# The second product of the last three token tiles by Strassen's scheme, with the order of work behind it placed anew

## The chip, the cores and the metric

The kernel runs on one core of a Trainium2 chip. The metric is device time in microseconds (us) of one launch. A core has engines that work side by side, each with a queue of its own in program order: PE (TensorE, matrix products; its weight loads are listed as PEld), DVE (VectorE), ACT (ScalarE), POOL (GpSimd) and SP (SyncE, here only an issuer of DMAs). They share SBUF, from which they work; PE writes its results to the banks of PSUM.

## The reference

Local attention with a few global positions, and on its result a block of two dense layers. There are 8 batches, 8 heads, 576 positions, 64 columns a head:

```python
mask = (abs(pos[:, None] - pos[None, :]) <= 32) | is_global[:, None] | is_global[None, :]
scores = where(mask, scale * q @ k.T, -1e9)
attn = softmax(scores) @ v                    # [8, 8, 576, 64]
x = attn.transpose(0, 2, 1, 3).reshape(4608, 512)
h = x @ w_in                                  # 512 x 2048
g = softplus(h)
out = g @ w_out                               # 2048 x 512, float32
```

The second product, g @ w_out, is what the change is about.

## The kernel before

The 4608 tokens are worked in nine tiles m = 0 to 8 of TT = 512 tokens (`add_moe`). Attention runs ahead of them in 36 units n, four to a tile. One unit goes through all engines: scores on PE (tile s, L1128), mask added on DVE (st, L1132), row maximum on DVE (m, L1145), its subtraction on POOL (L1151), exponential on ACT (L1168), sum and reciprocal on DVE (sm L1175, rs L1177), the product with the reciprocal on POOL (pn<-st,rs, L1183), a transpose on DVE (pt, L1192). When the four transposes of a tile are there, PE makes the attention's result (xo, L1294, about 150 small matmuls), which ACT and DVE copy into xT (L777). Rows of global positions have a small product of their own (ov, L1052; odd).

Then comes the dense block of the tile. `first` (L1331) makes h in 16 groups of 4 matmuls of 512 columns, and `soft` on ACT (L1337) turns each group into a tile g of bf16, 128 of the 2048 inner values by 512 tokens. `second` (L1342) takes four blocks of 128 tokens; each block sums 16 matmuls of 512 columns in one PSUM bank, with a weight load of g ahead of each. `oev` (L777) copies the sums to SBUF (osb) on ACT or DVE, and `store` (L1354) writes 256 KB to DRAM: POOL's queue for tiles 0 to 5 (m < OWN), ACT's for tiles 6 to 8. The last block of tile 8 is done in two halves of 256 columns. Exponential and softplus each need ACT to load a table when it goes from one to the other.

The order of all this on each engine is no result of queues meeting at run time. The class `_Order` collects jobs with their dependencies, and `o.follow(ORDER)` gives each its place from a long tuple of numbers: a number divided by 5 is the job, its remainder the engine (PE, ACT, DVE, POOL, DMA). Each engine then runs its jobs strictly as they were placed, waiting on semaphores where a job's inputs come from another engine. So PE places matmuls of tile m's second product among those of tile m + 1's first one, and around xo. `run` also knows a flag `port=True`: a DVE job with it that is placed later than a POOL job is put behind it where their estimated times overlap; a POOL job is only looked at where it starts inside a DVE job that was placed already.

Of the kernel before, what the change touches and what calls it, by code (L numbers as in the profile page):

```python
# [334 lines left out]
def kernel(  # L335
# [984 lines left out]
    def add_moe(m, exps):  # L1320
        nt = TT

        def lo_of(c, n):
# [14 lines left out]

        def second(e, ns, kf, a, z):
            if kf == 0:  # L1340
                PS["o", m, ns, a] = psum(("o", m, ns, a), [P, z - a], FP32)
            nc.tensor.matmul(out=PS["o", m, ns, a][:, :], lhsT=PS["g", m, kf][:, ns * P:(ns + 1) * P],  # L1342
                             rhs=w_out_t[kf // 4][:, kf % 4, a:z], start=(kf == 0), stop=(kf == KF - 1))
# [178 lines left out]
```

## Time and profile before

| | |
|---|---|
| median of 3 runs | 327.88 us (326.84 to 328.69) |
| span of the profiled execution | 325.7 us |
| between that span and the median | 2.2 us |
| TensorE busy, granted clock | 97% of the span, 1.000 |
| VectorE, ScalarE, GpSimd busy | 69%, 71%, 62% |
| matmuls in all, of them of the second product | 5099, 592 |

The profile is of one execution; it has no time of its own besides its span, which counts from the first instruction to the last, so what a launch has around that is in the 2.2 us. Matmuls are pipelined, and a PE that is shown as busy is not therefore at its peak. The releaser of a wait is the engine whose signal came last. A slice of the page is a fortieth of the span, 8.1 us; tile 6 begins with its xo at 228.9 us, tile 7 at 261.6, tile 8 at 289.4, and the last matmul ends at 322.6.

### The profile page before, as it was taken

The page shows a single profiled execution, that of the slowest core. Times are in us where ns is not written, and L with a number is a line of the kernel's source. Part 1 is how long each engine was busy: PE and PEld are TensorE (multiplying, and loading weights), DVE is VectorE, ACT ScalarE, POOL GpSimd, SP SyncE. Part 2 cuts the span into 40 slices and gives each one's busy share as a digit, 9 for nine tenths or more (in the row PEclk, how much of TensorE's full clock was granted, in tenths as well). Part 3 has the DMA queues.
Part 4 walks back from the last instruction along what each step waited for, and adds up shares of the span by engine and source line. Part 5 has one row for each costly group of instructions (what it writes and reads, how often), then busy time and mean ns, then how long its engine had stood idle before and what let it go on. Part 6 is the DMA issues. An engine that isn't in the chain of part 4 may idle for free.

```text
span 325.7 us, 11720 instructions
## 1 busy us (share of the span) xinstructions
PE 315.4 (97%) x5099; PEld 174.8 (54%) x5099; DVE 225.9 (69%) x399; ACT 231.1 (71%) x471; POOL 200.6 (62%) x182
## 2 busy tenths in 40 slices
PE   8887999989999999999999999999999999999996
PEld 7556974565565655544455445445544454454453
DVE  6898479994899799988687978678755792530000
ACT  7897784768599787789558964695789468824621
POOL 8980759974678498596759962988556428420000
PEclk9999999999999999999999999999999999999999
DMA  8999799999887999999960899440202101000112
GB/s 211 160 176 223 171 192 162 173 214 201 137 138 125 173 189 169 221 176 175 194 132 36 158 156 192 107 137 10 94 0 99 47 24 64 0 34 34 64 38 92
DMA packets 168652, 41.52 MB, mean 127 GB/s; under 512 B 153114, under 2 KB 165658, under 8 KB 168602
## 3 DMA queue, kind: packets, MB, share of 16 engines
q1 hardware_dynamic: 151048, 25.96, 45.4%
q0 software_dynamic: 15680, 11.67, 19.7%
q10 hardware_dynamic: 1874, 3.15, 2.5%
q8 instruction: 40, 0.66, 0.9%
q14 instruction: 10, 0.08, 0.1%
HBM read 36.70 MB, written 9.44 MB: 142 GB/s over the span
## 4 chain that ended last, share of the span: by engine, by line
PE 72%; DMA 9%; DVE 9%; SPq 6%; POOL 2%; issue 1%; ACT 0%; POOLq 0%
PE o L1342 31%; PE h L1331 31%; SPq L494 5%; DMA wout<-in_moe_w_out_dram 4%; PE xo L1294 3%; DMA stage<-in_q_dram 3%; PE s L1128 3%; DMA stage<-in_k_dram 2%; PE ov L1052 2%; DVE m L1143 1%; DVE pt L1192 1%; PE pick L942 1%; DVE sm L1175 1%; DVE pn L1183 1%; POOL wout L1398 1%
## 5 line engine op out<-in xcount | busy, mean ns | idle before, releaser
L1342 PE MATMUL o<-wout,g 128*128 128x512 bf16 (+1 forms) x592 | 139.0, 374 | 0.0
L1331 PE MATMUL h<-xT,win 128*128 128x512 bf16 (+3 forms) x832 | 138.0, 314 | 0.7 <-DVE xT L777 0.4
L1337 ACT ACTIVATE g<-h 128x512 bf16<-128x512 f32 (+3 forms) x208 | 84.7, 481 | 32.1 <-PE h L1331 29.5
L1331 PEld LDWEIGHTS <-win 128*128 128x128 bf16 x832 | 70.3, 98 | 56.9 <-issue 1.6
L1342 PEld LDWEIGHTS <-g 128*128 128x128 bf16 x592 | 55.9, 98 | 61.0 <-issue 1.7
L1151 POOL TENSOR_TENSOR st<-st,m 128x1024 f32<-128x1024 f32 x32 | 60.4, 1898 | 34.1 <-DVE m L1145 34.0
L1183 POOL TENSOR_TENSOR pn<-st,rs 128x1024 bf16<-128x1024 f32 (+1 forms) x33 | 60.5, 1841 | 27.9 <-DVE rs L1177 20.2
L1132 DVE TENSOR_TENSOR st<-s,mask 128x512 f32<-128x512 f32 x64 | 41.0, 679 | 13.5 <-PE s L1128 13.4
L1175 DVE TENSOR_REDUCE sm<-st 128x8 f32<-128x1024 f32 x32 | 38.3, 1197 | 14.1 <-ACT st L1168 14.1
L1145 DVE TENSOR_REDUCE m<-st 128x8 f32<-128x1024 f32 x32 | 38.2, 1206 | 0.2
L1168 ACT ACTIVATE st<-st 128x1024 f32<-128x1024 f32 x32 | 33.1, 1054 | 6.2 <-POOL st L1151 6.0
L777 ACT COPY osb<-o 128x512 f32<-128x512 f32 (+1 forms) x28 | 16.1, 580 | 22.3 <-PE o L1342 20.1
L1192 DVE STREAM_TRANSPOSE pt<-pn 128x512 int32<-128x512 int32 x36 | 24.5, 688 | 9.0 <-POOL pn L1183 9.0
L777 ACT CAST xT<-xo 128x512 bf16<-128x512 f32 (+3 forms) x33 | 12.8, 458 | 20.1 <-PE xo L1294 20.1
L777 POOL CAST qk<-stage 128x1152 bf16<-128x1152 f32 (+2 forms) x14 | 17.2, 1248 | 8.6 <-PE xo L1294 7.9
L1337 ACT ACT_TABLE_LOAD x15 | 19.2, 1283 | 0.3
L1168 ACT ACT_TABLE_LOAD x14 | 18.0, 1283 | 0.2
L777 POOL CAST vb<-stage 128x1152 bf16<-128x1152 f32 x11 | 12.6, 1147 | 5.8 <-DMA stage<-in_v_dram 3.5
L774 POOL TENSOR_SCALAR qk<-stage 128x1152 bf16<-128x1152 f32 (+1 forms) x9 | 12.0, 1330 | 6.1 <-PE s L1128 3.7
L1354 POOL DMA_DIRECT2D out_dram<-osb x24 | 13.8, 574 | 3.0 <-DVE osb L777 1.6
L1294 PE MATMUL xo<-pt,vb 32*64 32x96 bf16 (+2 forms) x1328 | 14.1, 210 | 1.3 <-issue 1.3
L777 DVE CAST xT<-xo 128x512 bf16<-128x512 f32 (+3 forms) x19 | 9.9, 549 | 7.7 <-PE xo L1294 7.6
(128 smaller groups left out, 298.0 us busy)
## 6 DMA issues: line engine op xcount, KB each, us to landing
stage<-in_k_dram SPq DMA_DIRECT2D x48, 144.0 KB, 4.0
stage<-in_q_dram SPq DMA_DIRECT2D x48, 144.0 KB, 4.0
stage<-in_v_dram SPq DMA_DIRECT2D x48, 144.0 KB, 3.4
out_dram<-osb POOLq DMA_DIRECT2D x24, 256.0 KB, 3.4
out_dram<-osb ACTq DMA_DIRECT2D x11, 256.0 KB, 2.0
stage<-in_q_dram SPq DMA_DIRECT2D x4, 512.0 KB, 5.6
stage<-in_k_dram SPq DMA_DIRECT2D x4, 512.0 KB, 7.4
win<-in_moe_w_in_dram POOLq DMA_DIRECT2D x8, 256.0 KB, 6.4
```

The lines of the kernel that those rows point to most:

```text
L777: {"ACT": nc.scalar.copy, "DVE": V.tensor_copy, "POOL": nc.gpsimd.tensor_copy}[e](out, in_)
L1132: V.tensor_tensor(out=PS["st", n][:, h, :, :], in0=PS["s", n, h][:, :, :], in1=mask[:, h, j0:j0 + PB, :, :].rearrange("p j s i -> p j (s i ...
L1145: V.reduce_max(out=m[:], in_=flat(PS["st", n], h0, h1), axis=AX)
L1151: on(e).tensor_tensor(out=t, in0=t, in1=over(PS["m", n, y][:], SL * BL), op=OP.subtract)
L1168: nc.scalar.activation(out=t, in_=t, func=AF.Exp)
L1175: V.reduce_sum(out=sm[:], in_=flat(PS["st", n], h0, h1), axis=AX)
L1183: on(e).tensor_tensor(out=PS["pn", n][:, :, :, h0:h1].rearrange("p x s h -> p h x s"), in0=PS["st", n][:, h0:h1], in1=PS["rs", n, y][:].re ...
L1192: V.transpose(out=bass.AP(base.tensor, base.offset, ap=[list(base.ap[0]), [2 * STEP, PB // 2], [STEP + BL // 2, 2], [1, SL * BL]]), in_=PS ...
L1294: nc.tensor.matmul(out=PS["xo", v_, c][h * D:(h + 1) * D, (x - X0) * BL:(z - X0) * BL], lhsT=lhs, rhs=rhs, start=start, stop=stop)
L1331: nc.tensor.matmul(out=h[:, :], lhsT=w_in_t[c // 4][:, kd, c % 4 * P:(c % 4 + 1) * P], rhs=PS["xT", m][:, kd, lo:hi], start=(kd == 0), sto ...
L1337: nc.scalar.activation(out=PS["g", m, c][:, lo:hi], in_=PS[key][:, lo_of(c, hi - lo)], func=AF.Softplus)
L1342: nc.tensor.matmul(out=PS["o", m, ns, a][:, :], lhsT=PS["g", m, kf][:, ns * P:(ns + 1) * P], rhs=w_out_t[kf // 4][:, kf % 4, a:z], start=( ...
```

## The change

For tiles 6, 7 and 8 (m >= FAST = 6) the second product is cut into quarters: the 512 tokens in two halves, the 2048 inner values in two halves y of 1024, the 512 output columns in two halves. Instead of the eight products of quarters, seven are made, of sums and differences of quarters, by Winograd's form of Strassen's scheme:

- Of w_out: T0 to T3 in bf16, each in two halves p of 128x1024, once for all three tiles. They lie in the staging buffers of q and k, which are free when the last batch is cast. Four of these eight operations are on DVE, four on POOL.
- Of g: S1 to S4, each in two halves p, for every tile. S1 goes to the staging buffer of v, S3, S2 and S4 overwrite quarters of g. S3 overwrites a quarter that S1 reads, S2 overwrites one that S3 reads and needs S1, S4 reads S2: a chain S1, S3, S2, S4. S2 waits besides for product 1, which reads the quarter that S2 overwrites, and S4 for product 2. Of the 24, 16 are on DVE, 8 on POOL.
- Each of the seven products (L1444 in the new file) is 16 matmuls of 256 columns, 8 inner steps by 2 blocks of tokens. Products 1, 6, 7, 4 add up in one PSUM bank, which is copied out after each of them (four evictions on ACT or DVE); product 2 has a bank, 5 and then 3 a third one, and three operations on DVE (`total`, L1469) add them from PSUM onto the copied sums. Product 1 needs no S; 5 needs S1, 6 S2, 7 S3, 3 S4; 5, 6, 7, 4 need T0 to T3.
- Stores of these tiles go through SP's queue as 256 tokens by 256 columns (256 KB, pieces of 1 KB).
- g is one tile of 16 parts instead of 16 tiles, with the same waits part by part.
- The order is kept for the first 3438 matmuls on PE; from about 189.8 us of the profile before on, every job is placed anew.

```diff
@@ ORDER
-        6527, 5817, 5185, 5470, 4588, 7249, 5475, 5480, 5190, 5762, 5768, 5195, 5200, 5681, 5485, 5726, 6437, 5732, 5205, 5738, 5375, 5821, 5140, 5210,
+        6527, 5817, 5185, 5470, 4588, 7304, 5475, 5480, 5190, 5762, 5768, 5195, 5200, 5681, 5485, 5726, 6437, 5732, 5205, 5738, 5375, 5821, 5140, 5210,
...
-    gp = ctx.enter_context(tc.tile_pool(name="moe_g", bufs=1))
+    gs_ = const([P, KF, TT], BF16, "g")
...
-        for ns in range(nt // P):
+        if m >= FAST:
+            add_fast(m, own[0])
+        for ns in range(nt // P if m < FAST else 0):
...
+    FAST = 6
+    KH, NH, DH = KF // 2, TT // 2, d_model // 2
+    fast = [flat(stage[w]).bitcast(BF16)[:, y * KH * DH:(y + 1) * KH * DH].rearrange("p (k n) -> p k n", k=KH) for w in range(2) for y in range(2)]
+    s1 = flat(stage[2]).bitcast(BF16)[:, 0:KH * NH].rearrange("p (k n) -> p k n", k=KH)
...
+    def combine(e, out, a, b, op):
+        on(e).tensor_tensor(out=out, in0=a, in1=b, op=op)
...
+        cost = {"DVE": (620, 700), "POOL": (1905, 1905)}
...
+        bank_of = {1: "a", 6: "a", 7: "a", 4: "a", 2: "b", 5: "c", 3: "c"}
...
+            for n in range(2):
+                nc.tensor.matmul(out=PS[key][:, n, :], lhsT=A[i](k, slice(n * P, (n + 1) * P)), rhs=Bs[i](k), start=i in new and k == n == 0, stop=k == KH - 1 and n == 1, skip_group_check=i not in new)
...
+        def total(e, i, x):
+            V.tensor_tensor(out=PS["osb", m, i][:], in0=PS["o", m, x][:], in1=PS["osb", m, i][:], op=OP.add)
+            send(i)
...
+            nc.sync.dma_start(out=out[n0:n0 + NH, c * DH:(c + 1) * DH].rearrange("(n p) d -> p n d", p=P), in_=PS["osb", m, i][:])
...
+            add_s(1, p, lambda e, p=p: combine(e, sp(p), gq(p, 0, 1), gq(p, 1, 1), SUB), lo + hi, g(0, p) + g(1, p) + ([("s1", m)] if p else []),
+                  [] if p else [("s1", ("s1", m))])
+            add_s(3, p, lambda e, p=p: combine(e, gq(p, 0, 1), gq(p, 0, 1), gq(p, 0, 0), SUB), [S_[1, p]], g(0, p))
+        u1 = add_evict(0, add_product(1, []))
+        add_total(0, "b", [add_product(2, []), u1])
+        for p in range(2):
+            add_s(2, p, lambda e, p=p: combine(e, gq(p, 0, 0), gq(p, 0, 0), sp(p), SUB), [S_[3, p], P_[1, 4 * p + 3]], g(0, p) + [("s1", m)])
+            add_s(4, p, lambda e, p=p: combine(e, gq(p, 1, 0), gq(p, 1, 0), gq(p, 0, 0), SUB), [S_[2, p], P_[2, 4 * p + 3]], g(0, p) + g(1, p))
```

In PE's own order the seven products of tiles 6 and 7 are still spread: products 1, 2 and part of 5 among the tile's own h groups or behind them, 6 and 7 between the last h and the next tile's xo, 4 and 3 behind that. Tile 8 has all seven behind its last h group: product 1, then pieces of 5 and 2, 6, the rest of 2, 7, 5, most of 4, 3, the end of 4.

Three places of the new order matter. The first is DVE after tile 6's h, up to the attention that tile 7 waits for. A row is the line, the operation and its tiles (lines are lower by one or shifted in the new file: L1176 is L1175 of before). It was, before:

```order
L1175 TENSOR_REDUCE sm<-st 128x8
L1177 RECIPROCAL rs<-sm 128x8
L1070 TENSOR_TENSOR odd<-ov,odd 128x129
L1072 RECIPROCAL grs<-odd 128x1
L1192 STREAM_TRANSPOSE pt<-pn 128x2x2x128
L1175 TENSOR_REDUCE sm<-st 128x8
L1177 RECIPROCAL rs<-sm 128x8
L1192 STREAM_TRANSPOSE pt<-pn 128x2x2x128
L1132 TENSOR_TENSOR st<-s,mask 128x512 x4
L1145 TENSOR_REDUCE m<-st 128x8
L1192 STREAM_TRANSPOSE pt<-pn 128x2x2x128
```

There every row belongs to the attention. It is now, with stage_62 as the place of S1 and L1402 as the line of the new sums:

```order
L1176 TENSOR_REDUCE sm<-st 128x8
L1178 RECIPROCAL rs<-sm 128x8
L1402 TENSOR_TENSOR stage_62<-g 128x1024
L1402 TENSOR_TENSOR g<-g 128x4x256
L1402 TENSOR_TENSOR stage_62<-g 128x1024
L1402 TENSOR_TENSOR g<-g 128x4x256
L1402 TENSOR_TENSOR g<-g,stage_62 128x4x256
L1193 STREAM_TRANSPOSE pt<-pn 128x2x2x128
L1176 TENSOR_REDUCE sm<-st 128x8
L1178 RECIPROCAL rs<-sm 128x8
L778 COPY odd<-ov 64x129 x2
L1193 STREAM_TRANSPOSE pt<-pn 128x2x2x128
```

Five S of tile 6 (two S1, two S3, one S2) stand in one row ahead of a transpose and of the sum and reciprocal from which POOL's last pn of the tile is made. On POOL stood, at the same place before:

```order
L1151 TENSOR_TENSOR st<-st,m 128x1024
L1354 DMA out_dram<-osb 128x512 x2
L1183 TENSOR_TENSOR pn<-st,rs 128x2x512
L1354 DMA out_dram<-osb 128x512
L1183 TENSOR_TENSOR pn<-st,rs 128x2x512 x2
L1151 TENSOR_TENSOR st<-st,m 128x1024 x4
```

and now:

```order
L1152 TENSOR_TENSOR st<-st,m 128x1024
L1353 DMA out_dram<-osb 128x512
L1184 TENSOR_TENSOR pn<-st,rs 128x2x512
L1402 TENSOR_TENSOR g<-g,stage_62 128x4x256
L1184 TENSOR_TENSOR pn<-st,rs 128x2x512 x2
L1402 TENSOR_TENSOR g<-g 128x4x256
L1152 TENSOR_TENSOR st<-st,m 128x1024
L1353 DMA out_dram<-osb 128x512
L1402 TENSOR_TENSOR g<-g 128x4x256
```

An S2 (g<-g,stage_62) now stands between two pn, and two S4 behind them. The third place is DVE from tile 7's S to the end of the next attention:

```order
L1402 TENSOR_TENSOR stage_62<-g 128x1024
L1402 TENSOR_TENSOR g<-g 128x4x256
L1193 STREAM_TRANSPOSE pt<-pn 128x2x2x128
L778 COPY osb<-o 128x512
L1402 TENSOR_TENSOR stage_62<-g 128x1024
L1402 TENSOR_TENSOR g<-g 128x4x256
L1402 TENSOR_TENSOR g<-g,stage_62 128x4x256
L1176 TENSOR_REDUCE sm<-st 128x8
L1178 RECIPROCAL rs<-sm 128x8
L1193 STREAM_TRANSPOSE pt<-pn 128x2x2x128
L1469 TENSOR_TENSOR osb<-o,osb 128x512
L1193 STREAM_TRANSPOSE pt<-pn 128x2x2x128
```

Here too the sum and reciprocal for the last pn of tile 8's attention stand behind S, and two transposes behind those.

More of the change, by code (lines that the diff above doesn't have):

```diff
@@ L740 @@
         SLOTS[f"g{c}"] = 1
+    SLOTS["s1"] = 1
     KINDS = dict(h=(4, 0), o=(3, 0), o0=(4, 0), s=(4, 0), tr=(4, 0), pick=(2, 0), sg=(2, 0), ov=(2, 0), xo=(4, 0), gi=(1, 0))
@@ L1334, in soft @@
         def soft(e, c, key, lo, hi):
-            if lo == 0:
-                PS["g", m, c] = gp.tile([P, nt], BF16, tag=f"g{c}", name=f"g{c}")
-            nc.scalar.activation(out=PS["g", m, c][:, lo:hi], in_=PS[key][:, lo_of(c, hi - lo)], func=AF.Softplus)
+            nc.scalar.activation(out=gs_[:, c, lo:hi], in_=PS[key][:, lo_of(c, hi - lo)], func=AF.Softplus)
         def second(e, ns, kf, a, z):
@@ L1341, in second @@
                 PS["o", m, ns, a] = psum(("o", m, ns, a), [P, z - a], FP32)
-            nc.tensor.matmul(out=PS["o", m, ns, a][:, :], lhsT=PS["g", m, kf][:, ns * P:(ns + 1) * P],
+            nc.tensor.matmul(out=PS["o", m, ns, a][:, :], lhsT=gs_[:, kf, ns * P:(ns + 1) * P],
                              rhs=w_out_t[kf // 4][:, kf % 4, a:z], start=(kf == 0), stop=(kf == KF - 1))
@@ new lines, in add_sums @@
+    def add_sums():
+        cost = {"DVE": (620, 700), "POOL": (1905, 1905)}
+        SUB, ADD = OP.subtract, OP.add
+        t = lambda y, p: fast[y][:, 4 * p:4 * p + 4, :]
+        for p in range(2):
+            deps = had(("w_out", p), ("w_out", 2 + p))
+            for y, (a, b, op) in enumerate(((lambda p: wq(p, 0, 1), lambda p: wq(p, 0, 0), SUB), (lambda p: wq(p, 1, 1), lambda p: t(0, p), ADD),
+                                            (lambda p: wq(p, 1, 1), lambda p: wq(p, 0, 1), ADD), (lambda p: wq(p, 1, 0), lambda p: t(1, p), SUB))):
+                T["T", y, p] = o.add(cost, lambda e, y=y, p=p, a=a, b=b, op=op: combine(e, t(y, p), a(p), b(p), op),
+                                     deps + ([T["T", 0, p]] if y == 1 else [T["T", 1, p]] if y == 3 else []), rank=60, port=True)
@@ new lines, in add_fast, with gq, sp, product @@
+    def add_fast(m, mine):
+        if ("T", 0, 0) not in T:
+            add_sums()
+        SUB = OP.subtract
+        cost = {"DVE": (620, 700), "POOL": (1905, 1905)}
+        N = slice(0, NH), slice(NH, 2 * NH)
+        def gq(p, y, x):
+            return gs_[:, y * KH + 4 * p:y * KH + 4 * p + 4, N[x]]
+        def sp(p):
+            return s1[:, 4 * p:4 * p + 4, :]
+        g = lambda y, p: [("g", m, y * KH + 4 * p + k) for k in range(4)]
+        A = {1: lambda k, n: gs_[:, k, n], 2: lambda k, n: gs_[:, KH + k, n], 3: lambda k, n: gs_[:, KH + k, n],
+             4: lambda k, n: gs_[:, KH + k, slice(NH + n.start, NH + n.stop)], 5: lambda k, n: s1[:, k, n],
+             6: lambda k, n: gs_[:, k, n], 7: lambda k, n: gs_[:, k, slice(NH + n.start, NH + n.stop)]}
+        Bs = {1: lambda k: wq(k // 4, 0, 0)[:, k % 4], 2: lambda k: wq(k // 4, 1, 0)[:, k % 4], 3: lambda k: wq(k // 4, 1, 1)[:, k % 4],
+              4: lambda k: fast[3][:, k], 5: lambda k: fast[0][:, k], 6: lambda k: fast[1][:, k], 7: lambda k: fast[2][:, k]}
+        bank_of = {1: "a", 6: "a", 7: "a", 4: "a", 2: "b", 5: "c", 3: "c"}
+        new = (1, 2, 5)
+        used = {1: 0, 2: 1, 3: 1, 4: 1, 5: None, 6: 0, 7: 0}
+        P_ = {}
+        S_ = {}
+        def product(i, k):
+            key = ("o", m, bank_of[i])
+            if i in new and k == 0:
+                PS[key] = psum(key, [P, 2, DH], FP32)
+            for n in range(2):
+                nc.tensor.matmul(out=PS[key][:, n, :], lhsT=A[i](k, slice(n * P, (n + 1) * P)), rhs=Bs[i](k), start=i in new and k == n == 0, stop=k == KH - 1 and n == 1, skip_group_check=i not in new)
+        def add_product(i, after):
+            key = ("o", m, bank_of[i])
+            last = None
+            for k in range(KH):
+                deps = list(after) if last is None else [last]
+                deps += {1: lambda: [mine["soft", k], T["w_out", k // 4]], 2: lambda: [mine["soft", KH + k], T["w_out", 2 + k // 4]],
+                         3: lambda: [S_[4, k // 4]], 4: lambda: [mine["soft", KH + k], T["T", 3, k // 4]], 5: lambda: [S_[1, k // 4], T["T", 0, k // 4]],
+                         6: lambda: [S_[2, k // 4], T["T", 1, k // 4]], 7: lambda: [S_[3, k // 4], T["T", 2, k // 4]]}[i]()
+                last = o.add(mm(2, DH), lambda e, i=i, k=k: product(i, k), deps, rank=6, ins=4, opens=[("o", key)] if i in new and k == 0 else [],
+                             uses=([] if i in new and k == 0 else [key]) + ([("s1", m)] if used[i] is None else [("g", m, used[i] * KH + k)]))
+                P_[i, k] = last
+            return last
+        def add_s(i, p, fn, deps, uses, opens=()):
+            T["S", m, i, p] = S_[i, p] = o.add(cost, fn, deps, rank=10 * m + 2, port=True, uses=uses, opens=opens)
+        def evict(e, i):
+            PS["osb", m, i] = op.tile([P, 2, DH], FP32, tag="osb", name="osb")
+            copy(e, PS["osb", m, i][:], PS["o", m, "a"][:])
+            if i == 3:
+                send(i)
+        def total(e, i, x):
+            V.tensor_tensor(out=PS["osb", m, i][:], in0=PS["o", m, x][:], in1=PS["osb", m, i][:], op=OP.add)
+            send(i)
+        def send(i):
+            r, c = ((0, 0), (0, 1), (1, 1), (1, 0))[i]
+            n0 = m * TT + r * NH
+            nc.sync.dma_start(out=out[n0:n0 + NH, c * DH:(c + 1) * DH].rearrange("(n p) d -> p n d", p=P), in_=PS["osb", m, i][:])
+        def add_evict(i, dep):
+            return o.add(either(512), lambda e: evict(e, i), [dep], rank=3, opens=[("osb", ("osb", m, i))], uses=[("o", m, "a")])
+        def add_total(i, x, deps):
+            return o.add({"DVE": dve(512)}, lambda e: total(e, i, x), deps, rank=3, uses=[("osb", m, i), ("o", m, x)])
+        for p in range(2):
+            lo, hi = ([mine["soft", y * KH + 4 * p + k] for k in range(4)] for y in range(2))
+            add_s(1, p, lambda e, p=p: combine(e, sp(p), gq(p, 0, 1), gq(p, 1, 1), SUB), lo + hi, g(0, p) + g(1, p) + ([("s1", m)] if p else []),
[3 more added lines that the diff above has]
+        add_total(0, "b", [add_product(2, []), u1])
+        for p in range(2):
+            add_s(2, p, lambda e, p=p: combine(e, gq(p, 0, 0), gq(p, 0, 0), sp(p), SUB), [S_[3, p], P_[1, 4 * p + 3]], g(0, p) + [("s1", m)])
+            add_s(4, p, lambda e, p=p: combine(e, gq(p, 1, 0), gq(p, 1, 0), gq(p, 0, 0), SUB), [S_[2, p], P_[2, 4 * p + 3]], g(0, p) + g(1, p))
+        u2 = add_evict(1, add_product(6, [u1]))
+        u3 = add_evict(2, add_product(7, [u2]))
+        T["second", m] = add_evict(3, add_product(4, [u3]))
+        c22 = add_total(2, "c", [add_product(5, []), u3])
+        add_total(1, "c", [add_product(3, [c22]), u2])
@@ L1489 @@
         make_batch(batches(us)[-1] + 1)
-    o.follow(ORDER)
+    for key in list(T):
+        if key[0] == "T":
+            T[key]["deps"] += T["cast", B - 1, 0] + T["cast", B - 1, 1]
+        elif key[0] == "S" and key[2] == 1:
+            T[key]["deps"] += T["cast", B - 1, 2]
+    if ORDER:
+        o.follow(ORDER)
     for job in o.run(dict(PE=1200 if WARM else 3000, ACT=2600, DVE=2100, POOL=3400, DMA=2000)):
```

2 lines of the change are left out of this document (added), and 54 rows, old and new, of the table ORDER.

## The prediction

> **What bounds the kernel now.** I read the page's busy shares and its 40 slices first, then the chain of waits in order of time, then busy time by stage.
>
> ```profile
> span 325.7 us, 11720 instructions
> PE 315.4 (97%) x5099; PEld 174.8 (54%) x5099; DVE 225.9 (69%) x399; ACT 231.1 (71%) x471; POOL 200.6 (62%) x182
> PE   8887999989999999999999999999999999999996
> DVE  6898479994899799988687978678755792530000
> POOL 8980759974678498596759962988556428420000
> PE 72%; DMA 9%; DVE 9%; SPq 6%; POOL 2%; issue 1%; ACT 0%; POOLq 0%
> ```
>
> TensorE is busy 97% of the span and carries 72% of the chain; the change works from slice 23 on, where PE stands at 9 throughout while VectorE and GpSimd stand at 5 to 9 until tile 8 begins. Other engines' work is free there as long as PE never waits for it.
>
> ```profile
> 189.78 5.50 PE o L1342 x25
> 300.98 6.04 PE h L1331 x28
> 309.62 13.00 PE o L1342 x74
> 322.62 0.02 issue
> 322.64 0.37 ACT osb L777
> ```
>
> ```profile
> L1342 PE MATMUL o<-wout,g 128*128 128x512 bf16 x46 | 10.4, 379 | 0.0
> L1342 PE MATMUL o<-wout,g 128*128 128x256 bf16 x28 | 3.5, 273 | 0.0
> ```
>
> The first fence is the chain: a matmul of 512 columns every 6.04/28 = 0.2157 us. The second groups the matmuls after 309.6 by shape: the 74 of the chain's 13.00 us are 46 of 512 columns and 28 of 256. 46 x 0.2157 = 9.92, so the 28 took 3.08, 0.110 each. If half the columns were exactly half the time, it would be 0.108.
>
> ```profile
> 190.00:230.00 40.00, 40.00 (x669) 19.80 (x669) 30.60 (x50) 26.17 (x42) 27.09 (x20) 1.00 0.58 122
> 230.00:262.00 32.00, 32.00 (x433) 15.09 (x419) 21.63 (x36) 22.55 (x33) 18.85 (x14) 1.00 0.14 51
> 262.00:290.00 28.00, 28.00 (x361) 13.54 (x334) 14.87 (x21) 20.23 (x29) 13.76 (x8) 1.00 0.08 29
> ```
>
> These are stages of the end (stretch, length, then busy time of PE, PEld, DVE, ACT, POOL, granted clock, DMA share, GB/s). From 190 to 290 DVE has 33 us free and POOL 40 of 100, so the 40 new operations fit by their sum. The question is whether the last one before a product, or before the next tile's attention, ends in time.
>
> **What the matmuls save.** A tile's second product was 64 x 0.2157 = 13.80 us; it becomes 112 matmuls of 256 columns, 12.32 at 0.110 or 12.10 at 0.108. That is 1.5 to 1.7 a tile, 4.4 to 5.2 for three (tile 8 had 32 of its matmuls halved already, which changes nothing at this pitch). I take -4.9. The number of weight loads rises by 128 with the matmuls; at 98 ns each
>
> ```profile
> L1342 PEld LDWEIGHTS <-g 128*128 128x128 bf16 x592 | 55.9, 98 | 61.0 <-issue 1.7
> ```
>
> they stay under 0.108, and PEld is under half busy: 0, covered by the matmuls themselves.
>
> **Waits that go.** The small pieces of PE's work in that stretch:
>
> ```profile
> 195.28 1.56 PE xo L1294 x146
> 261.68 1.59 PE xo L1294 x153
> 222.08 0.80 PE L1052 MATMUL ov<-vb,pgt 32*32 32x129 bf16 x72
> 222.81 3.63 PE L1342 MATMUL o<-wout,g 128*128 128x512 bf16 x16
> 254.86 0.75 PE L1128 MATMUL s<-kx,qx 64*32 64x128 bf16 x64
> ```
>
> From 189.78 to the end at 322.64 the order has 279 matmuls of 512 columns at L1342 (60.2), 32 of 256 (3.5), 256 of L1331 (55.2), four xo groups (6.4), 288 scores s (3.0 at the last row's pace, less its drain), two ov (0.73 each, 222.08 to 222.81) and small picks (about 1.4): 131.2 of 132.9. So 1.3 to 1.7 us are waits spread over that stretch; they lie at the places where I now count whole new waits, and I take -1.3.
>
> **The combinations.** 8 T once, 24 S (8 a tile), each 128x1024 bf16 out of two bf16 tiles in SBUF; 20 on DVE, 12 on POOL. No such instruction is in the trace. Nearest rows:
>
> ```profile
> L1183 DVE TENSOR_TENSOR pn<-st,rs 128x512 bf16<-128x512 f32 x5 | 3.4, 718 | 0.0
> L1151 POOL TENSOR_TENSOR st<-st,m 128x1024 f32<-128x1024 f32 x32 | 60.4, 1898 | 34.1 <-DVE m L1145 34.0
> L777 DVE COPY kx<-qkg 128x320 bf16<-128x320 bf16 x2 | 0.5, 243 | 0.1
> L1183 DVE TENSOR_TENSOR pn<-st,rs x2: 1274/1898/2522, 65.8 to 67.0; 128x1024 bf16<-128x1024 f32 x2
> L777 POOL CAST qk<-stage x14: 403/1469/2477, 7.9 to 207.5; 128x1152 bf16<-128x1152 f32 x9, 128x512 bf16<-128x512 f32 x4, 128x256 bf16<-128x256 f32 x1
> ```
>
> On POOL: 1.90. On DVE: at most 1.27, the fp32 operation of the same 1024 columns at its fastest; the bf16 copy of 320 columns at 0.24 says that narrow types can go at more than double pace, about 0.5 for 1024. I take 0.70, nearest to the fp32 row with half the columns, which moves as many bytes. The Trainium skill gives the same for two-input bf16 operations ("VectorE: DVE Perf Modes", The perf-mode tier table): twice the pace of fp32, 1224 ns for 2048 columns; by it an estimate of 0.69; no row here shows it.
>
> **The port.** The decisive price is what these cost beside each other. Before shows DVE and POOL working at once on operations with two SBUF operands:
>
> ```profile
> 65.79 3.69 DVE L1183 TENSOR_TENSOR pn<-st,rs 128x1024 bf16<-128x1024 f32 x2
> 66.57 4.20 POOL L777 CAST qk<-stage 128x1152 bf16<-128x1152 f32 x2
> ```
>
> From 65.79 to 70.77, 4.98 us, lie two DVE operations of 1.27 alone and two POOL casts of 1.47 alone. 4.98 - 2.55 = 2.43: they took turns, and each cast kept DVE out for about 1.22 of its 1.47 (one DVE operation shows 2.52 instead of 1.27). So an S on DVE beside a POOL operation of 1.9 costs up to 1.9 - 0.25 = 1.65, and POOL waits 0.70 in turn. The lower bound is nothing, where the starts don't cross; the upper 1.9. The rule of the Trainium skill ("SBUF — State Buffer", SBUF: two separate sides) is that a two-input DVE operation and a GpSimd operation share a port pair, which is locked for the whole instruction; the trace agrees on the turns, but shows 1.22 of 1.47. By the whole-instruction rule each turn costs 0.25 more, and the sum below would come about 1.5 us higher.
>
> **Where PE then waits.** So far only softplus stood between a tile's h and its second product. In the new order on DVE the S of tile 6 stand in front of the sum, reciprocal and transpose of the next tile's attention, with the POOL products pn between. Rows for these:
>
> ```profile
> L1183 POOL TENSOR_TENSOR pn<-st,rs 128x1024 bf16<-128x1024 f32 x30 | 57.0, 1902 | 27.1 <-DVE rs L1177 19.4 <-DVE kx L777 3.0 <-DVE odd L1070 2.7
> L1175 DVE TENSOR_REDUCE sm<-st 128x8 f32<-128x1024 f32 x32 | 38.3, 1197 | 14.1 <-ACT st L1168 14.1
> L1177 DVE RECIPROCAL rs<-sm 128x8 f32<-128x8 f32 x32 | 6.5, 203 | 1.1
> L1192 DVE STREAM_TRANSPOSE pt<-pn 128x512 int32<-128x512 int32 x36 | 24.5, 688 | 9.0 <-POOL pn L1183 9.0
> ```
>
> T: four on DVE and four on POOL between 209 and 233, where POOL is two thirds busy. The stage row of 190 to 230 has POOL at 27.1 of 40: most of it is hidden, and one turn of 0.7 may reach the chain: +0.5 (0 to 0.9).
>
> Tile 6, counted from the last h matmul of the tile. PE has 64 matmuls of 256 columns (7.0) and ov (0.7) until xo of tile 7: 7.7 of cover. On the way to xo: softplus 0.8; S1, S3 in turn with a POOL pn until 2.0; a POOL S2 1.65; S3 0.7; POOL pn 1.65; S2 0.7 (6.7); transpose 0.7; sum and reciprocal 1.4 (8.8); the last pn 1.9 and its handover 0.15; transpose 0.7: 11.6. Wait 3.9. Without turns it is about 8.0: 0.3.
>
> Tile 7, same place before xo of tile 8: cover 7.1. From 0.4 on: S1 0.7, S3 0.7, POOL S2 1.9, S1 0.7, pn 1.65, S3 0.7, S2 0.7, sum and reciprocal 1.4, pn 2.05, transpose 0.7: 11.6. Wait 4.5; without turns 8.2, so 1.1.
>
> Tile 8: nothing else is left for PE. Product 1 (16 matmuls, 1.7) covers the first S1, 24 matmuls (2.6 to 3.2) the first S2; POOL's S3 of 1.9 takes a turn between: 1.4 (0 to 2.5). POOL's S4, 1.9 twice, have until product 3, some 10 us: 0.
>
> The products end in evictions and totals on ACT and DVE (0.6 to 0.7 each), with a bank free meanwhile: 0 inside. Queues: the twelve stores go to SP, where nothing else is left behind them; POOL's queue is not passed by any.
>
> **The tail.**
>
> ```profile
> 323.04 0.34 ACTq L1354 DMA_DIRECT2D out_dram<-osb  x1
> L777 ACT COPY osb<-o 128x512 f32<-128x512 f32 x26 | 15.4, 596 | 19.0 <-PE o L1342 16.8 <-issue 1.3 <-ACT odd L777 0.8
> out_dram<-osb ACTq DMA_DIRECT2D x11, 256.0 KB, 2.0
> out_dram<-osb POOLq DMA_DIRECT2D x24, 256.0 KB, 3.4
> ```
>
> Before: last matmul 322.64, eviction of 256 columns 0.37, issue 0.34, landing 2.0. After: eviction of 512 columns 0.60 (+0.23), two 256 KB stores one behind the other on SP (+0.34), and lines of 1 KB instead of 2 KB: +0.3, between 0 and the 1.4 by which POOL's stores land later than ACT's. Together +0.9 (0.2 to 2.0).
>
> **Sum** against the profiled span of 325.7: -4.9 - 1.3 + 0.5 + 3.9 + 4.5 + 1.4 + 0.9 = +5.0, a span of 330.7. The median of the runs, 327.88, is 2.2 above the span, which I leave: 332.9 us.
>
> **Rivals.**
>
> *The turns don't fall so (faster).* If DVE's S slip in before POOL's operations, or a pn has already ended, the waits are 0 + 0.3 + 1.1 + 0 = 1.4: -4.9 - 1.3 + 1.4 + 0.9 = -3.9, 324.0. For it: DVE and POOL have 33% and 40% free, and PE at 9 in every slice shows that the present order leaves it no waits with the same engines crossing. It decides where all of the POOL operations beside S cost DVE less than some 5 us; against it, in the one overlap that the trace shows plainly, the two engines took strict turns. Chance 0.30.
>
> *Half of it.* Half of the turns: waits 1.4 + 4.45 = 5.85, sum +0.55, 328.4. Chance 0.18, of which most within 0.5% (1.64 us, about what a measurement of this kernel can tell from no change).
>
> *256 columns don't pay.* If each 256-column matmul took the 3.5/28 = 0.125 us of busy time in its row, because weight loads of 0.098 with what goes around them set the pace, 304 more of them cost what 176 of 512 columns did: no saving, +9.9, 337.8. Against it are the 13.00 us of the chain; for it that only 28 in a row were seen. Chance 0.08. An S of 1.27 on DVE instead of 0.70 would end near there as well: four to five of them in the chains of tiles 6 and 7 each, about +5 in all.
>
> **The numbers.** Forecast (+2.5 to +8) 0.44, half 0.18, faster 0.30, no saving 0.08. Within 0.5%: 0.14 of the half and 0.03 from the faster case's edge, 0.17; faster by more: 0.29; slower: 0.54. Eight in ten: leaving out 0.11 of the faster case below 323.5 and the larger part of the no-saving case above 337.0.
>
> **What would show it.** In the changed kernel's profile: 336 matmuls of 256 columns in runs of 0.110 or less (step 1); S on DVE at 0.7 where POOL is idle, and some at over 2 us where it isn't (the port); PE idle before xo, put down to the DVE transpose, once for tile 7 and once for tile 8, 3 to 5 us each; an idle piece within the last products; 0.9 us more between the last matmul and the span's end. I am wrong if S on DVE show 0.7 throughout beside busy POOL, or if PE still stands at 9 in the slices from 23 on; then 324 is near.

## Result and the profile after

The changed kernel takes 336.3 us (median; 334.3 to 336.8) against 328.0 before: a ratio of 1.0247, 95% interval 1.0201 to 1.0292. A fourth execution fell into a slower state of the chip (342.9 us at a clock of 0.973); it and such executions of the kernels below are left out of the medians. The kernel is slower, as forecast, by 8.3 us where 5.0 were forecast: just beyond the +8 of the forecast case, inside the range. The profiled span is 334.2 us, 8.5 more than before.

The page of the changed kernel, lines as they were read of before:

```profile
span 334.2 us, 12019 instructions
PE 309.8 (93%) x5185; PEld 188.2 (56%) x5227; DVE 260.2 (78%) x428; ACT 235.4 (70%) x473; POOL 225.8 (68%) x193
PE   7888999989999999999999999999995999599984
PE 66%; DVE 22%; POOL 4%; ACT 3%; issue 2%; DMA 1%; POOLq 0%; DVEq 0%
```

PE is busy for 5.6 us less and the kernel is longer. (Some 2.9 of the 5.6 lie ahead of tile 5's xo, where the work is the same; this trace has 5227 weight loads and records of only 5185 of their matmuls.) Two slices, about 251 to 259 and 284 to 292 us, fall to 5, and DVE's share of the chain goes from 9% to 22%. The timeline of PE shows what it waits for there (start, length, matmuls, in brackets the idle time ahead and who ended it):

```profile
253.38 0.61 PE L1444 MATMUL o<-stage,stage 128*128 128x256 bf16 x4 [0.79 <-DVE stage L1402]
258.21 3.40 PE L1444 MATMUL o<-stage,g 128*128 128x256 bf16 x16 [3.35 <-DVE g L1402]
262.54 1.91 PE L1444 MATMUL o<-stage,g 128*128 128x256 bf16 x16
264.38 0.41 PE L1295 MATMUL xo<-pt,vg 32*64 32x448 bf16 x8
289.01 0.61 PE L1444 MATMUL o<-stage,g 128*128 128x256 bf16 x4 [1.07 <-POOL g L1402]
292.59 1.05 PE L1444 MATMUL o<-stage,g 128*128 128x256 bf16 x8 [2.09 <-DVE g L1402]
296.74 0.43 PE L1295 MATMUL xo<-pt,vg 32*64 32x512 bf16 x8
319.08 0.61 PE L1444 MATMUL o<-stage,stage 128*128 128x256 bf16 x4 [1.61 <-DVE stage L1402]
```

All of the long waits are for sums (L1402): in tiles 6 and 7 in front of product 5 and in front of or inside product 6, in tile 8 in front of product 5; xo itself waits for nothing. Product 7 of tile 6, 16 matmuls in 1.91 with their drain of 0.16, has the pace of 0.109 that was forecast. Product 6 just before it needed 3.40. The answer by stretches (length, PE busy, granted clock, DMA share, GB/s) says why:

```profile
256.00:258.00 2.00, 0.00 (x0) 0.96 0.00 0
258.00:260.00 2.00, 1.79 (x9) 0.50 0.00 0
260.00:262.00 2.00, 2.00 (x15) 0.68 0.00 0
262.00:264.00 2.00, 2.00 (x21) 1.00 0.12 42
```

Some 3.0 us into the wait of 3.35, PE got half its clock, and kept it for 3.4 us. And the sums, by line (count, shortest/median/longest in ns), with DVE and POOL side by side in tiles 6 and 8:

```profile
L1402 DVE TENSOR_TENSOR stage<-g x6: 684/1834/2637, 249.8 to 316.4; 128x1024 bf16<-128x1024 bf16 x6
L1402 POOL TENSOR_TENSOR g<-g x6: 2118/2129/2409, 262.1 to 323.5; 128x1024 bf16<-128x1024 bf16 x6
253.36 2.50 DVE L1402 TENSOR_TENSOR g<-g 128x1024 bf16<-128x1024 bf16 x1
252.87 2.44 POOL L1402 TENSOR_TENSOR g<-g,stage 128x1024 bf16<-128x1024 bf16 x1 [1.43 <-DVE g L1402]
316.39 2.64 DVE L1402 TENSOR_TENSOR stage<-g 128x1024 bf16<-128x1024 bf16 x1 [0.17 <-ACT g L1336]
316.36 2.12 POOL L1402 TENSOR_TENSOR g<-g 128x1024 bf16<-128x1024 bf16 x1 [18.33 <-DVE stage L1402]
```

A sum on DVE is 0.68 to 0.69 alone and up to 2.64 beside POOL: at 316.39 it was kept out for 2.64 - 0.69 = 1.95 of POOL's 2.12. What keeps it out is called the port here, as in the prediction.

For most kernels below, the time between the first matmuls of each xo, from there to the start of the last eviction on ACT, and on to the end of the span (us, from each profile's timeline; up to tile 5's xo the work is the same in all, and that xo begins up to 3.9 us apart, so the last column is the fairer comparison of profiles). A profile is of one execution, not of the median one: that of "clock kept (26 short)" is the slowest of five (340.9; the others took 336.2 to 337.5), that of "pn on DVE" the fastest (338.0).

| kernel | xo 5 to 6 | 6 to 7 | 7 to 8 | xo 8 to last eviction | to the end | sum |
|---|---|---|---|---|---|---|
| before | 33.64 | 32.76 | 27.77 | 33.26 | 3.06 | 130.5 |
| changed | 34.50 | 35.09 | 32.36 | 33.06 | 4.40 | 139.4 |
| no sums S | 34.50 | 29.35 | 28.39 | 31.24 | 4.36 | 127.8 |
| DVE's sums as transposes | 34.41 | 29.35 | 28.52 | 31.25 | 4.44 | 128.0 |
| S1 to S3 on DVE | 34.50 | 34.39 | 32.96 | 31.57 | 4.39 | 137.8 |
| clock kept (26 short) | 34.51 | 33.82 | 35.98 | 33.06 | 4.41 | 141.8 |
| clock kept (12 + 8 long) | 34.50 | 33.82 | 33.31 | 33.05 | 4.34 | 139.0 |
| S1 to S3 and pn on DVE | 34.51 | 33.06 | 36.73 | 31.58 | 4.37 | 140.3 |
| pn on DVE | 34.49 | 34.08 | 35.13 | 33.06 | 4.37 | 141.1 |

### The profile page after: what moved, and what is told of

It reads as the page before. It is cut to its first block, busy times and chain, and to the rows that moved or that the text cites. A ratio compares the mean times of both kernels' runs of the same rounds, so it can differ in the third digit from the quotient of the medians.

```text
span 334.2 us, 12019 instructions
## 1 busy us (share of the span) xinstructions
PE 309.8 (93%) x5185; PEld 188.2 (56%) x5227; DVE 260.2 (78%) x428; ACT 235.4 (70%) x473; POOL 225.8 (68%) x193
## 4 chain that ended last, share of the span: by engine, by line
PE 66%; DVE 22%; POOL 4%; ACT 3%; issue 2%; DMA 1%; POOLq 0%; DVEq 0%
PE h L1332 31%; PE o L1341 17%; PE o L1444 7%; PE xo L1295 4%; DVE sm L1176 3%; DVE stage L1402 3%; DVE g L1402 3%; PE s L1129 2%; DVE st L1133 2%; DVE m L1146 2%; DVE pt L1193 2%; DVE pn L1184 2%; POOL vb L499 1%; DMA vb<-in_v_dram 1%; PE ov L1053 1%
## 5 line engine op out<-in xcount | busy, mean ns | idle before, releaser
L1332 PE MATMUL h<-xT,win 128*128 128x512 bf16 (+3 forms) x820 | 135.7, 313 | 1.5 <-DVE xT L778 0.4
L1341 PE MATMUL o<-wout,g 128*128 128x512 bf16 x358 | 86.8, 379 | 2.5 <-issue 2.1
L1184 POOL TENSOR_TENSOR pn<-st,rs 128x1024 bf16<-128x1024 f32 (+1 forms) x33 | 61.5, 1870 | 29.5 <-DVE rs L1178 24.4
L1341 PEld LDWEIGHTS <-g 128*128 128x128 bf16 x384 | 36.0, 98 | 40.3 <-issue 1.2
L1176 DVE TENSOR_REDUCE sm<-st 128x8 f32<-128x1024 f32 x32 | 38.3, 1198 | 6.5 <-ACT st L1169 6.5
L778 ACT COPY osb<-o 128x512 f32<-128x512 f32 x25 | 14.7, 593 | 33.7 <-PE o L1444 25.3
L1444 PEld LDWEIGHTS <-g 128*128 128x128 bf16 x288 | 28.2, 100 | 13.8 <-DVE g L1402 6.0
L1402 POOL TENSOR_TENSOR g<-g 128x1024 bf16<-128x1024 bf16 x6 | 13.0, 2174 | 21.0 <-DVE stage L1402 18.3
L1444 PE MATMUL o<-stage,g 128*128 128x256 bf16 x144 | 19.7, 288 | 6.5 <-DVE g L1402 5.4
L778 ACT CAST xT<-xo 128x512 bf16<-128x512 f32 (+3 forms) x34 | 13.5, 463 | 16.4 <-PE xo L1295 16.4
L1444 PE MATMUL o<-wout,g 128*128 128x256 bf16 x144 | 20.0, 273 | 0.0
L1402 DVE TENSOR_TENSOR stage<-g 128x1024 bf16<-128x1024 bf16 x6 | 9.9, 1647 | 11.4 <-ACT g L1336 11.3
```

The lines of the kernel that those rows point to most:

```text
L778: {"ACT": nc.scalar.copy, "DVE": V.tensor_copy, "POOL": nc.gpsimd.tensor_copy}[e](out, in_)
L1176: V.reduce_sum(out=sm[:], in_=flat(PS["st", n], h0, h1), axis=AX)
L1184: on(e).tensor_tensor(out=PS["pn", n][:, :, :, h0:h1].rearrange("p x s h -> p h x s"), in0=PS["st", n][:, h0:h1], in1=PS["rs", n, y][:].re ...
L1332: nc.tensor.matmul(out=h[:, :], lhsT=w_in_t[c // 4][:, kd, c % 4 * P:(c % 4 + 1) * P], rhs=PS["xT", m][:, kd, lo:hi], start=(kd == 0), sto ...
L1341: nc.tensor.matmul(out=PS["o", m, ns, a][:, :], lhsT=gs_[:, kf, ns * P:(ns + 1) * P], rhs=w_out_t[kf // 4][:, kf % 4, a:z], start=(kf == 0 ...
L1402: on(e).tensor_tensor(out=out, in0=a, in1=b, op=op)
```

## Experiments

The theory: DVE's two-input sums and POOL's operations exclude each other, so the sums come late, PE stands, and loses its clock besides. The rivals: half-width matmuls or the new order cost the time by themselves; or DVE is just too full in front of the attention.

**The sums left out.**

```diff
-            ... = o.add(cost, fn, deps, rank=10 * m + 2, port=True, ...)
+            ... = o.add(cost, lambda e: None, deps, rank=10 * m + 2, port=True, ...)
-             4: ..., 5: lambda k, n: s1[:, k, n],
+             4: ..., 5: lambda k, n: gs_[:, KH + k, slice(NH + n.start, NH + n.stop)],
```

> The 24 sums S of g are left out: the same 336 matmuls in the same order read the raw quarters of g (the T stay), so the result is another one. Theory (PE waits for S, and S waits for the port): the waits of 0.8, 3.35, 0.4, 1.1, 2.1 and 1.6 us go, with them the time at half clock (1.7) and the later attention; the pace of 0.108 us stays. Some 11 of the 13.7 us by which PE's work now exceeds its pitch go: 325 to 327 us, a little below before. Rival (half-width matmuls with 128 more weight loads, or the new order by itself, cost the time): stays at 332 or above.

325.9 us; ratio to before 0.9949 (0.9908 to 0.9990). The 336 matmuls, their loads, T, the new order and the tail together are no slower than before: that rival falls. It does not yet tell waiting for the port from waiting for work.

**DVE's sums as transposes.**

```diff
     def combine(e, out, a, b, op):
+        if e == "DVE":
+            i32 = lambda x: x.bitcast(I32)
+            V.transpose(out=i32(out), in_=i32(b))
+            return
         on(e).tensor_tensor(out=out, in0=a, in1=b, op=op)
```

> Every sum that runs on DVE (16 S, 4 T) becomes a DVE transpose of the same 128x1024 bf16 tile, one input instead of two, into the same place, waited for by the same matmuls (another result). POOL's sums stay as they are. Theory (the two-input operations take turns with POOL at a shared port): the transposes take 0.65 to 0.70 us each beside a busy POOL, where nine of the sums took 1.6 to 2.6; PE's waits shrink by about 4.9 us of stretched sums in tile 6, 3.9 in tile 7, 1.9 in tile 8, less what POOL's own S2 keeps: 327 to 330 us. Rival (DVE simply has five operations more in front of the attention, port or no port): the chain keeps its length, 335 to 337.

324.8 us; 0.9893 (0.9833 to 0.9953), below even the range of the theory. Groups by line and shape (count, then busy time, mean ns):

```profile
L1404 DVE STREAM_TRANSPOSE stage<-g 128x512 int32<-128x512 int32 x6 | 4.2, 694 | 11.5 <-ACT g L1336 11.4
L1404 DVE STREAM_TRANSPOSE g<-g 128x512 int32<-128x512 int32 x6 | 4.1, 682 | 0.4 <-PE o L1448 0.4
258.19 0.40 PE L1295 MATMUL xo<-pt,vg 32*64 32x448 bf16 x8 [0.15 <-DVE pt L1193]
```

The same number of DVE operations, of the same size, in the same rows, with POOL's sums left as they were, cost nothing: xo of tile 7 comes at 258.2 instead of 264.4, and the table has 128.0 us, as with no sums at all (127.8). Not DVE's length but its two-input operations beside POOL cost 139.4 - 128.0 = 11.4 us, half clock included: 5.7 in tile 6, 3.8 in tile 7, 1.8 in tile 8. A transpose differs from a sum in its type too, but the type is not needed for the effect: the fp32 pn of the prediction's rows, with two inputs as well, took 2.52 beside POOL where it takes 1.27.

**S1 to S3 on DVE.**

```diff
+            if i != 4:
+                fn = lambda e, fn=fn: fn("DVE")
             T["S", m, i, p] = S_[i, p] = o.add(cost, fn, deps, ...)
```

> The three of S1 to S3 that POOL does (one S2 of tile 6, one of tile 7, one S3 of tile 8) go to DVE; S4 and T stay. The result is the same. Theory (port): each takes 0.7 on DVE instead of 2.1 to 2.4 on POOL with the turns that it forces; DVE still takes turns with POOL's pn. 331 to 334 us. Rival (DVE is the overloaded engine there): one operation more in DVE's row per tile, 337 to 339.

334.5 us; 1.0203 (1.0134 to 1.0271), just over the theory's range; its interval does not part it from the changed kernel's. Tile 8, where no pn is left, gains 1.5 (33.06 to 31.57). Tile 6 gains only 0.7, tile 7 loses 0.6. The timeline of tile 6:

```profile
249.99 4.05 DVE L1402 TENSOR_TENSOR stage<-g 128x1024 bf16<-128x1024 bf16 x1
249.72 3.76 POOL L1184 TENSOR_TENSOR pn<-st,rs 128x1024 bf16<-128x1024 f32 x2
256.21 0.82 PE L1444 MATMUL o<-stage,stage 128*128 128x256 bf16 x4 [3.43 <-DVE stage L1402]
```

With POOL's S2 gone from between them, two pn follow each other, and DVE's sum sits out both. This is not the rule. In the changed kernel an S2 and a pn of POOL follow each other in tile 7, and there DVE's sum came in between:

```profile
286.83 2.12 POOL L1402 TENSOR_TENSOR g<-g,stage 128x1024 bf16<-128x1024 bf16 x1 [1.42 <-DVE g L1402]
288.91 2.35 POOL L1184 TENSOR_TENSOR pn<-st,rs 128x1024 bf16<-128x1024 f32 x1
287.81 1.69 DVE L1402 TENSOR_TENSOR stage<-g 128x1024 bf16<-128x1024 bf16 x1
```

It ended 0.55 behind the S2, and the pn took 2.35 instead of 1.90. So it was in tile 6 too (at 255.3), and in tile 7 of this kernel (at 284.9). Why it was otherwise at 251.6 stays open.

**The clock kept in tile 6.**

```diff
+            if (m, i, k) == (FAST, 6, 0):
+                for _ in range(26):
+                    nc.tensor.matmul(out=PS[key][:, 0, :], lhsT=idle[:, 0:P], rhs=idle[:, 0:DH], start=False, ...)
             for n in range(2):
```

> In the wait of 3.35 us before tile 6's product 6, PE does 26 matmuls of 256 columns with weights of zero onto the same sums (2.8 us at full clock). The result is the same. Theory: the granted clock stays at 1.00 where it was 0.50 to 0.68 for 3.4 us behind the wait, so product 6 takes 1.75 us instead of 3.4: about 1.6 us less, 334.5 to 335.5. Rival (the clock there is not due to the idle time, or the waiting chain is what ends last anyway): no change, 336.5.

337.3 us; 1.0267 (1.0192 to 1.0341): no gain.

```profile
260.84 1.92 PE L1447 MATMUL o<-stage,g 128*128 128x256 bf16 x16 [0.51 <-DVE g L1402]
269.52 0.49 PE L1447 MATMUL o<-stage,g 128*128 128x256 bf16 x3 [1.90 <-issue]
296.00:298.00 2.00, 1.98 (x13) 0.66 0.00 0
298.00:300.00 2.00, 2.00 (x11) 0.50 0.00 0
```

The mechanism is right: product 6 takes 1.92 instead of 3.40, and tile 6 is 1.3 us shorter. Tile 7 gives back 3.6: a wait of 1.9 for which the profile shows no releaser (issue), and half clock at 296, behind tile 7's wait. This profile is of the slowest execution, so the 3.6 need not be in the others; but they show no gain either (336.2 to 337.5).

**The clock kept in both tiles.**

```diff
+            fill = {(6, 6, 0): 12, (7, 6, 4): 8}.get((m, i, k), 0)
+            for _ in range(fill):
+                nc.tensor.matmul(out=PS[key][:], lhsT=idle[:, 0:P], rhs=idle[:, 0:2 * DH], start=False, ...)
```

> The changed kernel with zero-weight matmuls of 512 columns in PE's wait before product 6 of tile 6 (12 of them, 2.6 us) and in that inside product 6 of tile 7 (8, 1.7 us); 20 matmuls instead of the 26 of the first try, 512 columns each. The result is the same. Theory: the first try saved 1.3 us in tile 6 and lost them to half clock in tile 7 and to 1.9 us of a wait for PE's own instructions. With both waits filled the granted clock stays at 1.00 in both, and 1.3 to 1.6 us come out: 334.7 to 335.5 against 336.5. Rival (the time saved in tile 6 only makes PE wait longer before tile 8's attention, whose chain on DVE and POOL sets the end): 336 to 337, with the clock at 1.00.

334.7 us; 1.0218 (1.0148 to 1.0288): at the lower edge of what was expected, but the interval does not part it from the changed kernel. In the profile the clock stays at 1.00 in both waits and tile 6 again gains 1.3, but tile 7 loses 0.95:

```profile
262.50 0.40 PE L1295 MATMUL xo<-pt,vg 32*64 32x448 bf16 x8 [0.15 <-DVE pt L1193]
266.79 1.46 PE L1332 MATMUL h<-xT,win 128*128 128x512 bf16 x6 [0.78 <-ACT st L1169]
```

With PE earlier, xo just meets the attention's last transpose, and h waits for ACT, which it had not done. Of the clock's 1.5 us (half of the time from 258.21 to 261.27 in the changed kernel) some 0.4 come out in the sum of the profiles; the rest is covered by the next chain. The medians differ by 1.6 (336.3 to 334.7), and the changed kernel's fastest execution, 334.3, has a mean clock of 0.998 where the two others have 0.993, so it seems to have escaped half clock. How much the clock is worth in the end stays open between these.

**pn to DVE as well, and pn alone.**

```diff
+            if n > 7 * TP and n % TP:
+                e = "DVE"
             on(e).tensor_tensor(out=PS["pn", n]...
```

> S1 to S3 all on DVE, and with them the last three products pn of the attention of tiles 7 and 8 each (POOL's partners of the sums before). The result is the same. POOL keeps S4, T and the subtractions. Theory (DVE is kept out for whole POOL operations): no POOL operation is left beside the sums, so each takes 0.69 and each pn 1.27 on DVE; although DVE has some 11 us more to do, xo of tile 7 comes 3 us earlier, that of tile 8 another 2.5 to 3, tile 8's wait of 1.6 goes: 327.5 to 331 us. Rival (DVE's length is what counts): six pn and three sums more on the engine in front of xo, 338 or more.

> Only those six pn go to DVE; POOL keeps its S2 and S3. The result is the same. Theory: the sums are held up by POOL's own S2 and S3 alone (2.1 us each, once in tile 6 and 7, once in tile 8), not by pn: tile 6 and 7 gain 1.5 to 2.5 each, tile 8 nothing: 331.5 to 334. If POOL's S and not pn were the holder that counts, no gain: 336.

338.5 us, 1.0306 (1.0216 to 1.0396), and 340.8 us, 1.0372 (1.0283 to 1.0462). Both expectations were wrong. With sums and pn on DVE:

```profile
258.20 1.30 DVE L1186 TENSOR_TENSOR pn<-st,rs 128x1024 bf16<-128x1024 f32 x1
265.62 0.50 PE L1297 MATMUL xo<-pt,vg 32*64 32x448 bf16 x8 [2.52 <-DVE pt L1195]
266.00:268.00 2.00, 2.00 (x163) 0.50 0.19 59
291.94 2.31 DVE L1404 TENSOR_TENSOR stage<-g 128x1024 bf16<-128x1024 bf16 x1
291.59 2.12 POOL L1404 TENSOR_TENSOR g<-g 128x1024 bf16<-128x1024 bf16 x1 [2.63 <-DVE g L1404]
```

In tile 6 every sum takes 0.68 to 0.69 and the products wait once, 1.0 us; but pn, 1.3 each, now stand in DVE's row in front of the transposes, and xo waits 2.5 us and meets half clock. Tile 6 gains 2.0 in all. In tile 7 POOL, free earlier, starts its S4 at 291.59, just ahead of DVE's next S1, which takes 2.31: a new collision, worth 1.6. Tile 7 loses 4.4 against the changed kernel; the rest, beside three pn more in DVE's row, was not taken apart. With pn alone on DVE, POOL's S4 holds up a pn itself:

```profile
290.00 3.20 DVE L1186 TENSOR_TENSOR pn<-st,rs 128x1024 bf16<-128x1024 f32 x1
289.61 2.44 POOL L1404 TENSOR_TENSOR g<-g 128x1024 bf16<-128x1024 bf16 x1
```

So work taken from POOL and put on DVE is paid there: in these profiles the two engines do not overlap such work, and the rival (DVE's length) is right as soon as DVE has to do both engines' share.

**The last store on another queue** (on the kernel with S1 to S3 and pn on DVE).

```diff
-            nc.sync.dma_start(out=out[n0:n0 + NH, ...
+            (nc.scalar if i == 3 else nc.sync).dma_start(out=out[n0:n0 + NH, ...
```

> The kernel with S1 to S3 and six pn on DVE, with the store behind the last eviction of each tile on ACT's queue instead of SP's. Theory of the tail (after the last eviction, two stores of 256 KB are issued one behind the other and move 512 KB): the second one is issued at once, 0.3 to 0.4 us less than the same kernel with all stores on SP; that the 512 KB have to move stays. Rival (the transfer alone sets the tail): no difference.

337.7 us; 1.0312 (1.0244 to 1.0379), the same. From the last eviction to the end it has 4.64 us, the same kernel with all stores on SP 4.37. The queue is not it. The stretches of the changed kernel (length, busy of PE, PEld, DVE, ACT, POOL, clock, DMA share, GB/s) agree:

```profile
331.00:332.00 1.00, 0.00 (x0) 0.00 (x0) 0.00 (x0) 0.00 (x0) 0.00 (x0) 1.00 0.79 267
332.00:333.00 1.00, 0.00 (x0) 0.00 (x0) 0.00 (x0) 0.00 (x0) 0.00 (x0) 0.97 0.73 257
```

Two stores, 512 KB, move at 260 GB/s for two microseconds; before it was 128 KB.

**Strassen where nothing collides.** The experiments point to one place: in tile 8 no attention follows, and from its xo on POOL had nothing to do. This kernel has the scheme in tile 8 alone, in the order of before:

```diff
-    FAST = 6
+    FAST = 8
```

ORDER is that of before up to tile 8's xT. Behind it T is on DVE, the h groups are placed so that the first halves of S1 and S3 come 6 us ahead of the last one, all S are on DVE, product 3 is done by blocks of tokens, and its total and store are in two halves.

> Strassen's scheme in tile 8 alone, in the order of the kernel before: its last 85 jobs are replaced. T is made on DVE behind the last xT (DVE was busy 1.3 of 19 us there, POOL 0), all eight S on DVE, tile 8's h groups are put so that the first halves of S come before the last h group, and the last store is 128 KB. The result is the same. Theory (the sums cost nothing where no POOL operation stands beside them and no attention behind them): each S takes 0.69, PE does not wait, and the saving of one tile (64 x 0.2157 - 112 x 0.108 = 1.7 us) comes out whole, less up to 0.3 in the tail: 326 to 326.8, about 1.4 below before. Rival (the matmuls of 256 columns or their weight loads cost what they save): no difference, 327.9; rival (PE waits for S behind the last h all the same): 329 or more.

327.2 us against 327.5 beside it; 0.9990 (0.9954 to 1.0025): inside what the measurement can tell from no change. In the profile the last 85 jobs behave as the theory says:

```profile
302.83 0.69 DVE L1402 TENSOR_TENSOR stage<-g 128x1024 bf16<-128x1024 bf16 x1 [5.42 <-ACT g L1336]
312.69 1.92 PE L1445 MATMUL o<-stage,g 128*128 128x256 bf16 x16
321.64 0.76 DVE L1472 TENSOR_TENSOR osb<-o,osb 128x256 f32<-128x256 f32 x2 [2.75 <-PE o L1445]
```

Every sum takes 0.68 to 0.69. From xo of tile 8 to the release of the last total it is 31.94 us (289.70 to 321.64) where before had 33.26 to its last eviction: 1.3 of the 1.7 expected. The end takes 3.56 instead of 3.06. What is left, 0.8 in the profile, no timing here separates from nothing. By its time alone the rival (no difference) fits as well; its reason does not, since 16 matmuls of 256 columns took 1.92 with their drain of 0.16.

## Why the prediction came out as it did

**The saving of the matmuls** stood: 16 in 1.75 us, 0.109 each. The rival that 256 columns don't pay is out, by that row and by the kernel without sums. The 0.70 taken for a sum on DVE held as well (0.68 to 0.69 alone). Everything without the port was to give -3.9 (the faster case); with transposes it gave -2.5 (130.5 to 128.0). Of the 1.4 between them, 0.8 lie in the first stretch and 0.5 in the tail, the two steps that follow.

**T** was to cost 0.5 by the port. From xo 5 to xo 6 it is 0.86 longer than before, with transposes 0.77: the port takes 0.1 there, and the rest comes with the order placed anew, for which I had counted nothing; it was not taken apart.

**The tail** was to cost 0.9 and costs 1.34 (3.06 to 4.40). The step that failed: I counted the second store's issue, and the other queue changed nothing; what the stretches show is that 512 KB instead of 128 KB have to move. No run stores less at the end of the otherwise unchanged kernel, so this is read and not tested.

**The waits** were the decisive term: 10.3, of which 8.9 by the port (1.4 being what I gave the chains without it). Measured by the transposes, the port costs 11.4, with the half clock that it brings. The mechanism is shown; three of its steps were wrong:

- Place. I had PE wait in front of xo, for DVE's transpose. It waits in front of products 5 and 6, for the sums; xo comes late because PE is late. I had counted PE's products as cover for the attention's chain, though they hang on the same sums. So it is in part luck that the term of tile 7 comes near the measured one (below).
- Size of one turn. From casts of 1.47 that seemed to hold the port for 1.22, I took 1.65 for a POOL operation of 1.9. The 1.22 came out of a sum that holds the second cast too, which no two-input DVE operation waited for; the first one kept DVE out for 2.52 - 1.27 = 1.25. POOL's bf16 sums take 2.12, not 1.9, and one kept DVE out for 1.95; and turns are not strict (once a sum sat out two pn, 4.05 us). By the rule of the Trainium skill that I set beside my row ("SBUF — State Buffer", SBUF: two separate sides), the whole of POOL's instruction, I would have been nearer: 1.95 of 2.12.
- The clock. I gave PE's waits no cost beyond their length. In tile 6 half clock made 1.5 us of it: I had 3.9 there, of which 3.6 by the port, and 5.7 were measured; tile 7 (3.4 by the port) had 3.8, tile 8 (1.4) 1.8. But keeping the clock up gave only 0.4 in the sum of the profiles, so its cost can't simply be added to the wait's.

**The rivals.** The faster case, 324.0 if DVE and POOL did not hinder each other, was well sized: the kernel with transposes does just that and takes 324.8. Its condition was what failed.

## What to carry to other kernels

Before work is moved to idle engines, look at which of their operations can run at once: idle shares of 30 to 40% on DVE and POOL are not two reserves if both need the same port, and then one engine's length is added to the other's. Test that by putting one-input operations of the same size in place of the suspected ones: if the time goes, the port has it. And count as cover only matmuls that do not themselves wait for the chain they are to cover.

## What the runs showed of the hardware that was not expected

- DVE's two-input sums and POOL's operations shut each other out for most of an operation, and mostly in turn: where two POOL operations followed each other, a DVE operation that waited came in between in the overlap of before that the prediction shows, and in the changed kernel at 255.3 and 288.9 us. Once it did not: a sum, 0.69 alone, took 4.05 us beside two pn of 3.76 together.
- A DVE transpose of a 128x512 int32 tile takes 0.66 to 0.71 us beside a busy POOL, a two-input bf16 sum of 128x1024 up to 2.64 beside one POOL operation.
- Half clock is not decided by a wait's length alone. The changed kernel had it after its wait of 3.35 us, the kernel with 26 short matmuls after one of 2.09 in tile 7; with pn alone on DVE, a wait of 3.49 in tile 7 went without. While these kernels run, half clock comes in pieces of 3.41 us, and the times between its steps are multiples of that (71.7 us of full clock behind 261.27 in the changed kernel are 21). Laid on the trace, such pieces tell the three apart (two rows for each kernel, in the order just named; a row is a stretch, its length, PE busy, then PEld, DVE, ACT, POOL, the clock, DMA):

```profile
254.45:257.86 3.41, 0.41 (x4) 0.12 (x2) 3.38 (x2) 0.00 (x0) 3.16 (x2) 1.00 0.00 0
257.86:261.27 3.41, 3.06 (x15) 2.19 (x16) 3.30 (x7) 0.00 (x0) 0.98 (x1) 0.50 0.00 0
293.25:296.66 3.41, 1.32 (x13) 0.95 (x11) 3.38 (x3) 0.00 (x0) 1.45 (x1) 1.00 0.00 0
296.66:300.07 3.41, 3.41 (x18) 2.37 (x17) 2.19 (x5) 0.59 (x1) 2.59 (x2) 0.50 0.00 0
289.55:292.96 3.41, 1.48 (x12) 1.09 (x12) 3.41 (x2) 0.00 (x0) 2.44 (x1) 1.00 0.00 0
292.96:296.38 3.42, 1.83 (x17) 1.65 (x18) 3.35 (x7) 0.59 (x1) 0.00 (x0) 1.00 0.00 0
```

  A piece in which PE was busy for 1.32 us or less was followed by half clock, and the wait of 3.49 fell into two pieces that kept 1.48 and 1.83. That is where the line lies in these rows; PE's busy time alone need not be what decides. The Trainium skill ("TensorE: Matmul & The Clock Gate", Part 1: The HAM clock gate) has activity judged over windows of about 3.4 us that run freely, so that it depends on where a gap falls in them. All of these rows agree with that.
- 52 more instructions on PE in one place were followed by a wait of 1.9 us there that the profile puts down to PE's own issue; 40 in two places were not. They need not be its cause: such waits stand in other profiles too, 1.29 us at 32 us in before and 2.94 at 34 us in the kernel with S1 to S3 and pn on DVE. Why was not tried.
